# More rounds of filling products, one result copy on ScalarE, and the last value load in three pieces

## The chip, the cores and the metric

The kernel runs on one core of a Trainium2 chip. TensorE (PE in the profile) multiplies, and its weight loads are listed as PEld; VectorE (DVE), ScalarE (ACT) and GpSimd (POOL) work on tiles in on-chip memory; the sequencer of SyncE (SP) issues nearly all DMA transfers. Each engine has a sequencer of its own that also runs loop counters, register arithmetic, branches and semaphore waits; the profile gives its instructions a q (PEldq is TensorE's). The metric is the device time of one execution in microseconds (us). The kernel before takes 1368.91 us, the median of three runs from 1368.70 to 1369.06.

## The reference: two attention decodes

Two independent attentions, A and B, each for one new token in four sequences. Cut to what matters:

```python
def _A_ref(x, k_cache, v_cache, wq, wo):          # 32 query heads on 8 key heads
    q = (x @ wq) as (B, 32, 1, 128)
    k, v = the last W = 2048 positions of the caches, each head used four times
    p = softmax(q . k * 128 ** -0.5)
    return (p . v) as (B, 1, 4096) @ wo

def _B_ref(x, k_cache, v_cache, wq, wo):          # 32 heads, all 8192 positions
    q = (x @ wq) as (B, 32, 1, 128)
    p = softmax(q . k_cache * 128 ** -0.5)
    return (p . v_cache) as (B, 1, 4096) @ wo

return concatenate([a, b], axis=-1)               # (4, 1, 1024)
```

All inputs are bf16. B's two caches are by far the largest part of the bytes read.

## The kernel before

The work is cut into chunks. A has 8 chunks, each one key head for all four sequences. B has 32, each four heads of one sequence: 256 key tiles and 256 value tiles of 128 by 128, 8.4 MB of each. Here a chunk of B is called y, from 0 to 31. B's chunks 0, 4, 8, ... 28 begin a group of four that share one load of the output weights (`wos`, 0.5 MB).

The order of the work is written out by hand. `_Sched` keeps one list of operations for each engine, with the keys that each operation waits for. `emit_looped` finds equal stretches of a list and emits them as a hardware loop; on TensorE one such loop covers the chunks of B, so there is one copy of a B chunk in TensorE's program, and what differs from chunk to chunk is computed from the loop's register.

`whole_B` (L982) is one chunk of B on all engines. In order of TensorE:

- `reorder`: 16 products that bring the chunk's output weights from `wos` into the wanted order (in PSUM banks `tr` and `po`). `take_wol` copies them to `wol` with VectorE and ScalarE.
- `more_busy` (L947): the filling products, whose result (bank `sc`) nobody reads. A round is `BUSYBODY` = 3 products of 128 by 512. They stand in a loop of their own, a `Fori` whose end is an expression in the chunk's number (L961). That gives `MOREBUSY` + 1 = 4 rounds for y from 2 to 28 and one round for the others.
- For each of 32 groups of 8 key tiles, `emit_T` transposes the tiles (L519, `tr<-identb,kv`), VectorE or ScalarE copies them to `kt`, and two groups later `emit_S` multiplies them with the query (L521, `sc<-qq,kt`). The first group waits for the chunk's keys to land. Maxima and exponentials of the first half are put in between.
- `emit_pv`: 256 products of value tiles with probabilities, the first 128 into `po`, the other 128 into `tr`, with the statistics of the second half between them. At the tile groups listed in `QV` it waits for that part of the value tiles to have landed.
- `norm_sum`, `add_first`, `norm_out` and `emit_fin` scale the result and multiply it with the output weights (bank `fin`).

The loads are in one queue of SP (L498 to L504): for each chunk the keys, then the values, and after the last chunk two pieces of A's output weights (`dma_wo`, chunks 6 and 7 of A). The key buffer holds one chunk and the value buffer holds one chunk. The keys of chunk y + 1 are asked for when the first 128 key tiles of chunk y have been transposed; the values of chunk y + 1 when the value products of chunk y are done with that part. GpSimd passes on that a piece has landed (L85, `relay`) and copies half of a chunk's keys to a spare place (L440) in chunks whose keys come as one piece. Most loads are one piece of 256 tiles. Those of the last chunk are cut up: `LASTV` gives its values in pieces of 128, 64, 48 and 16 tiles.

After the last chunk, two products close bank `fin` for B, the last A chunks' products with the output weights follow, and `emit_out` (L891) copies each result from `fin` to `outsb` on VectorE and issues two output DMAs, one from ACT's queue and one from SP's. B's copy comes first, then A's last products, then A's copy.

Of the kernel before, what the change touches and what calls it, by code (L numbers as in the profile page):

```python
# [7 lines left out]
ACTF = mybir.ActivationFunctionType  # L8
# [21 lines left out]
QUARTERS = (64, 64, 64, 64)  # L30
NLATE = 4
NEXTV = (128, 64, 64)
LASTV = (128, 64, 48, 16)
QK = (0, 4, 8)
QC = (16, 24)
QV = (0, 8, 16, 24, 30)
NBUSY = 0
BUSYBODY = 3
MOREBUSY = 3
FILL = (6, 3)  # L40

TRM0, BC0, L0, Q0, XT0 = 0, 256, 288, 320, 448
# [146 lines left out]
def bass_concat_heads__sliding_block_cached__mha_block_cached__decode_kernel(  # L189
# [6 lines left out]
    DO = A_wo.shape[1]  # L196
# [33 lines left out]
    chunks.append(dict(chunks[NCA]))  # L230
    assert all(sum(x) == NTB for x in (LASTV, NEXTV, ENDK, QUARTERS, HALVES, WHOLE)) and NTA * 16 == 1024 and NTB * 4 == 1024
    NCP = (NTB - KMAIN) // TG

    sch = _Sched()
    with ExitStack() as es:
        block = es.enter_context(nc.Block())

        def sb(name, shape, dt):
            return es.enter_context(nc.sbuf_tensor(name, shape, dt))

        def ps(name, shape, dt):
            return es.enter_context(nc.psum_tensor(name, shape, dt))
# [38 lines left out]
        outsb = sb("outsb", [P, DO // 2], BF16)  # L281
# [9 lines left out]
        fin = ps("fin", [P, 512], F32)  # L291
# [22 lines left out]
            waits=["c_onesf", "c_identf"], key="c_ind")  # L314
# [85 lines left out]
        def vpieces(c):  # L400
            return LASTV if c == NC - 1 else NEXTV if c == NC - 2 else HALVES if c <= NCA + 2 or c == NC - 3 else WHOLE

# [64 lines left out]
        def land_vB(c):  # L467
# [3 lines left out]
            for i, m in enumerate(pieces):  # L471
                sch.relay("pool", sems, "r_v", m // TG, [("v", c, i)])
            for g, end in zip(QV, QV[1:] + (NTB // TG,)):
                sch.tk[("vr", c, g)] = ("r_v", n * (NTB // TG) + end)
# [290 lines left out]
        def emit_pv(c, g):  # L765
# [3 lines left out]
            for t in range(TG):  # L769
# [11 lines left out]
                if j == 0:  # L781
                    po_read[:] = []
                waits += [("vr", c, g)] if t == 0 and g in QV else []
                o = (po2 if h else po)[:, 0:NW]
# [103 lines left out]
        def out_halves(ab):  # L888
            return [(64 * (1 - ab) + 32 * h, slice(h * DO // 2, (h + 1) * DO // 2)) for h in (0, 1)]

        def emit_out(c):  # L891
            ab = 0 if c < NCA else 1
            at = out_halves(ab)
            rows = slice(at[0][0], at[1][0] + NB)
            sch.add("dve", lambda e: e.tensor_copy(outsb[rows, :], fin[rows, 0:DO // 2]), waits=[("end", 32) if ab else ("fin", c)], key=("osb", ab))
            for h, (p0, x) in enumerate(at):
                sch.add_dma("sp" if h else "act", lambda e, x=x, p0=p0: e.dma_start(out[:, 0, ab * DO + x.start:ab * DO + x.stop], outsb[p0:p0 + NB, :]),
                            "d_out", waits=[("osb", ab)], key=("out", ab, h))
# [48 lines left out]
        def more_busy(c):  # L947

            n = c - NCA

            def mm(e):
                return e.matmul(sc[:, 1, :], identb[:, :], sel4[:, :, :].rearrange("p r x -> p (r x)"), start=True, stop=True)  # L952

            def emit(e, x=0):
                if isinstance(e, _Record):
                    return mm(e)
                if isinstance(x, int):
                    for _ in range(BUSYBODY):
                        mm(e)
                    return None  # L960
                with nc.Fori(0, (((x + n + 30) >> 5) - ((x + n + 3) >> 5)) * MOREBUSY + 1, 1, engines=type(mybir.ALL_ENGINES)([mybir.EngineType.PE])):  # L961
                    for _ in range(BUSYBODY):
                        mm(e)
                return None

            sch.add("pe", emit, at=n)
# [96 lines left out]
        for c in range(NCA - LATEWO, NCA - 1):  # L1063
            emit_fin(c)
        emit_out(NC - 1)
        emit_fin(NCA - 1)
        emit_out(NCA - 1)

        @block.sync
# [56 lines left out]
```

## Time and profile before

| | |
|---|---|
| three timed runs, median | 1368.91 us |
| the profiled execution, its own time | 1368.63 us |
| its span, first to last instruction | 1366.9 us |
| mean granted TensorE clock | 0.984 |
| read from HBM | 587.21 MB |
| TensorE busy | 1222.5 us, 89% |
| VectorE, ScalarE, GpSimd busy | 731.2, 555.0, 202.8 us |
| filling products (L952), weight loads | 339, 30.6 us |

The profile shows one execution. Times in its views count from the first instruction; the execution's own time is 1.7 us longer than its span. A row of a timeline has the start, the length, the engine, the line of the program and what was written from what, with the idle time ahead of it and what ended that in brackets. `x` counts the instructions taken together. A row of one source line gives shortest, median and longest duration in ns, and the first and last start in us.

### The profile page before, as it was taken

The numbers are of one execution on the slowest core, as the hardware profiler recorded it, in microseconds if no ns is written. First come the engines' busy times: TensorE is split into PE (matmuls) and PEld (weight loads), VectorE is DVE, ScalarE is ACT, GpSimd is POOL, SyncE is SP. The second block draws the span as 40 slices with busy tenths as digits, with TensorE's granted clock in tenths as the row PEclk, the third lists the DMA queues.
The fourth block names the chain that finished last, engine by engine and source line by source line (L and its number), as shares of the span: only waits on it lengthen the run. The fifth ranks groups of instructions, "written<-read, shape, count | busy, mean of one in ns | idle before, by whom it ended". The sixth has DMA issues, their size and how long they took to land.

```text
span 1366.9 us, 62986 instructions
## 1 busy us (share of the span) xinstructions
PE 1222.5 (89%) x27834; PEld 1127.1 (82%) x27951; DVE 731.2 (53%) x1495; ACT 555.0 (41%) x777; POOL 202.8 (15%) x84
## 2 busy tenths in 40 slices
PE   6688799989998999989999899989999899999998
PEld 5688798878888988878889888878898888888888
DVE  2575355545555555545555555545555555455555
ACT  2353344334344443433444444334444343344443
POOL 2000022222210222222101222221022222200000
PEclk9998899999999999999999999999999999999999
DMA  9999999999999999999999999999999999999998
GB/s 398 427 428 431 430 439 432 438 433 428 433 433 426 441 433 433 426 432 443 432 430 430 441 432 432 432 433 435 433 432 430 439 433 432 430 439 420 433 424 368
DMA packets 16772, 587.51 MB, mean 430 GB/s; under 512 B 1880, under 2 KB 2032, under 8 KB 4208
## 3 DMA queue, kind: packets, MB, share of 16 engines
q1 hardware_dynamic: 16720, 587.21, 99.7%
q8 instruction: 15, 0.25, 0.1%
q14 instruction: 5, 0.04, 0.0%
q10 hardware_dynamic: 32, 0.01, 0.0%
HBM read 587.21 MB, written 0.01 MB: 430 GB/s over the span
## 4 chain that ended last, share of the span: by engine, by line
DMA 64%; PE 32%; DVE 1%; issue 1%; ACT 1%; SPq 0%; POOLq 0%; ACTq 0%; DVEq 0%
DMA kv<-in_B_k_cache_dram 58%; PE tr L519 20%; PE sc L521 9%; DMA kv<-in_A_k_cache_dram 4%; DMA kv<-in_B_v_cache_dram 3%; PE tr L521 2%; PE po L521 1%; PE ms L521 0%; DVE sA L649 0%; ACT pba L748 0%; PE sc L952 0%; ACT kt L594 0%; PE fin L521 0%; DVE kt L596 0%; ACT pbb L718 0%
## 5 line engine op out<-in xcount | busy, mean ns | idle before, releaser
L519 PE MATMUL tr<-identb,kv 128*128 128x128 bf16 x8704 | 662.1, 221 | 60.2 <-POOLq L85 49.8
L596 DVE COPY kt<-tr 128x1024 bf16<-128x1024 bf16 x736 | 502.2, 691 | 320.9 <-PE tr L519 317.8
L519 PEld LDWEIGHTS tr<-identb,kv 128*128 128x128 bf16 x8704 | 511.7, 99 | 77.0 <-issue 68.7
L594 ACT ACTIVATE kt<-tr 128x1024 bf16<-128x1024 bf16 x352 | 359.3, 1023 | 457.0 <-PE tr L519 454.8
L521 PE MATMUL sc<-qq,kt 128*128 128x64 bf16 x8192 | 398.9, 192 | 11.4 <-DVE kt L596 9.5
L521 PEld LDWEIGHTS sc<-qq,kt 128*128 128x128 bf16 x8192 | 327.9, 98 | 18.5 <-DVE kt L596 12.7
L440 POOL COPY kv<-kv 128x4096 int32<-128x4096 int32 x54 | 192.9, 3602 | 988.2 <-DMA kv<-in_B_k_cache_dram 988.2
L718 ACT ACTIVATE pbb<-sc,negb 32x128 bf16<-32x128 f32 x256 | 137.9, 539 | 134.2 <-DVE negb L700 131.4
L521 PE MATMUL tr<-pbb,kv 128*128 128x64 bf16 x4096 | 137.1, 194 | 27.1 <-ACT pbb L718 25.5
L521 PEld LDWEIGHTS tr<-pbb,kv 128*128 128x128 bf16 x4096 | 132.4, 100 | 30.9 <-issue 28.6
L521 PE MATMUL po<-pbb,kv 128*128 128x64 bf16 x4096 | 135.1, 194 | 2.9 <-issue 2.4
L521 PEld LDWEIGHTS po<-pbb,kv 128*128 128x128 bf16 x4096 | 127.5, 98 | 4.0 <-issue 2.5
L866 ACT ACTIVATE wol<-tr 128x512 bf16<-128x512 f32 x32 | 19.1, 597 | 201.4 <-PE po L521 201.4
L952 PE MATMUL sc<-sel,identb 128*128 128x512 bf16 x226 | 67.7, 381 | 9.5 <-issue 5.2
L868 DVE CAST wol<-tr 128x512 bf16<-128x512 f32 x64 | 41.2, 686 | 54.7 <-PE tr L521 54.7
L952 PEld LDWEIGHTS sc<-sel,identb 128*128 128x128 bf16 x339 | 30.6, 98 | 46.6 <-issue 14.2
L725 DVE TENSOR_REDUCE rs<-pbb 128x4 f32<-128x512 bf16 x32 | 22.0, 686 | 50.1 <-ACT pbb L718 50.1
L798 DVE RECIPROCAL ib<-ms 128x8 f32<-128x8 f32 x32 | 6.7, 208 | 58.8 <-PE ms L521 58.8
L521 PE MATMUL tr<-wos,back 32*128 32x512 bf16 x384 | 34.8, 383 | 0.5 <-issue 0.5
L521 PE MATMUL po<-wos,back 32*128 32x512 bf16 x128 | 33.9, 385 | 0.0
L686 DVE TENSOR_REDUCE gm<-ms 4x4 f32<-4x128 f32 x72 | 19.8, 275 | 25.0 <-PE ms L519 25.0
L666 DVE TENSOR_REDUCE rh<-sc 128x4 f32<-128x512 f32 x32 | 22.1, 692 | 14.3 <-PE sc L521 14.3
(90 smaller groups left out, 490.1 us busy)
## 6 DMA issues: line engine op xcount, KB each, us to landing
kv<-in_B_v_cache_dram SPq DMA_DIRECT2D x10, 4096.0 KB, 25.2
kv<-in_B_k_cache_dram SPq DMA_DIRECT2D x7, 4096.0 KB, 21.7
kv<-in_A_k_cache_dram SPq DMA_DIRECT2D x8, 2048.0 KB, 15.7
kv<-in_A_v_cache_dram SPq DMA_DIRECT2D x8, 2048.0 KB, 16.9
kv<-in_B_k_cache_dram SPq DMA_DIRECT2D x6, 2048.0 KB, 27.1
kv<-in_B_v_cache_dram SPq DMA_DIRECT2D x3, 2048.0 KB, 30.9
kv<-in_A_wq_dram SPq DMA_DIRECT2D x1, 4096.0 KB, 12.4
kv<-in_B_wq_dram SPq DMA_DIRECT2D x1, 4096.0 KB, 22.8
```

The lines of the kernel that those rows point to most:

```text
L440: sch.add("pool", lambda e, dst=dst, org=org: e.tensor_copy(dst, org), waits=[("T", s0 + ch["NG"] - 1)] if g == QC[0] else [])
L519: sch.add("pe", lambda e: e.transpose(o, l, r), waits, key)
L521: sch.add("pe", lambda e: e.matmul(o, l, r, start=start, stop=stop), waits, key)
L594: sch.add("act", lambda e: e.activation(dst, src, ACTF.Copy), waits=waits, key=("ev", s))
L596: sch.add("dve", lambda e: e.tensor_copy(dst, src), waits=waits, key=("ev", s))
L666: sch.add("dve", lambda e: e.tensor_reduce(out=dst, in_=src, axis=AX.X, op=ALU.max), waits=[("S", ch["s"] + (half + 1) * ch["NG"] // 2 - 1 ...
L686: sch.add("dve", lambda e: e.tensor_reduce(out=gm[0:C, m, 0:U], in_=src, axis=AX.X, op=ALU.max), waits=[key_of("trm", c, half)], key=key_o ...
L718: sch.add("act", lambda e, src=src, dst=dst, pp=pp, u=u: e.activation(dst, src, ACTF.Exp, bias=negb[pp, half, u:u + 1], scale=scale), wait ...
L725: sch.add("dve", lambda e: e.tensor_reduce(out=dst, in_=probs_of(c, half).rearrange("p j u -> p u j"), axis=AX.X, op=ALU.add), waits=[("ex ...
L866: sch.add("act", lambda e, u=u, o=o: e.activation(wol[:, u, :], o, ACTF.Copy), waits=[("reord", c, u)], key=("wol", c, u))
L868: sch.add("dve", lambda e, u=u, o=o: e.tensor_copy(wol[:, u, :], o), waits=[("reord", c, u)], key=("wol", c, u))
L952: return e.matmul(sc[:, 1, :], identb[:, :], sel4[:, :, :].rearrange("p r x -> p (r x)"), start=True, stop=True)
```

## The change: the diff

Three edits. The number of rounds of filling products goes from four to five for y from 2 to 28, and to seven for y = 4, 8, 12, 16, 20 and 24; the expression for the loop's end gets a second term, `first`, that is 1 for those six chunks and 0 for the others. B's result is copied to `outsb` by ScalarE; A's copy stays on VectorE. The last chunk's values come in three pieces of 128, 88 and 40 tiles, and the last place at which the value products wait moves from group 30 to group 27, in all chunks.

```diff
-LASTV = (128, 64, 48, 16)
+LASTV = (128, 88, 40)
...
-QV = (0, 8, 16, 24, 30)
+QV = (0, 8, 16, 24, 27)
...
-MOREBUSY = 3
+MOREBUSY = 4
+GROUPBUSY = 2
...
-            sch.add("dve", lambda e: e.tensor_copy(outsb[rows, :], fin[rows, 0:DO // 2]), waits=[("end", 32) if ab else ("fin", c)], key=("osb", ab))
+            waits = [("end", 32) if ab else ("fin", c)]
+            if ab:
+                sch.add("act", lambda e: e.activation(outsb[rows, :], fin[rows, 0:DO // 2], ACTF.Copy), waits=waits, key=("osb", ab))
+            else:
+                sch.add("dve", lambda e: e.tensor_copy(outsb[rows, :], fin[rows, 0:DO // 2]), waits=waits, key=("osb", ab))
...
-                with nc.Fori(0, (((x + n + 30) >> 5) - ((x + n + 3) >> 5)) * MOREBUSY + 1, 1, engines=type(mybir.ALL_ENGINES)([mybir.EngineType.PE])):
+                y = x + n
+                first = ((y >> 2) - ((y + 3) >> 2) + ((y + 31) >> 5) - ((y + 4) >> 5) + 33 >> 1) - 16
+                with nc.Fori(0, (((y + 30) >> 5) - ((y + 3) >> 5)) * MOREBUSY + first * GROUPBUSY + 1, 1, engines=type(mybir.ALL_ENGINES)([mybir.EngineType.PE])):
                     for _ in range(BUSYBODY):
                         mm(e)
```

## The prediction

> **What bounds the kernel now.** I read the page first, then the chain of waits.
>
> ```profile
> span 1366.9 us, 62986 instructions
> ...
> PEclk9998899999999999999999999999999999999999
> DMA  9999999999999999999999999999999999999998
> ...
> DMA 64%; PE 32%; DVE 1%; issue 1%; ACT 1%; SPq 0%; POOLq 0%; ACTq 0%; DVEq 0%
> ...
> 1118.47 28.08 DMA kv<-in_B_k_cache_dram
> 1157.17 28.07 DMA kv<-in_B_k_cache_dram
> ```
>
> The DMA engines are busy in every slice. A chunk's keys are asked for every 1157.17 - 1118.47 = 38.70 us, in which 16.8 MB of keys and values come in, 433 GB/s; they land 28 us after they are asked for, of which their own bytes need 19.4 us, so something is always queued ahead of them. The kernel before is bound by the transfers. The 32% of PE in the chain is the work that frees a buffer while the queue is still full.
>
> So the question is how far TensorE is from becoming the bound. The timeline of TensorE's weight loads and the chain give it, around an ordinary chunk (y = 27), one that begins a group (y = 24), and at y = 1 and 28:
>
> ```profile
> 1179.91 0.17 PEld L521 LDWEIGHTS tr<-wos,back 32*128 32x128 bf16 x6 [0.26 <-issue]
> ...
> 1185.41 1.34 PEld L519 LDWEIGHTS tr<-identb,kv 128*128 128x128 bf16 x24 [2.19 <-issue]
> ...
> 1218.61 0.16 PEld L521 LDWEIGHTS tr<-wos,back 32*128 32x128 bf16 x6 [0.26 <-issue]
> ...
> 1062.52 0.17 PEld L521 LDWEIGHTS tr<-wos,back 32*128 32x128 bf16 x6 [0.26 <-issue]
> ...
> 1069.30 1.34 PEld L519 LDWEIGHTS tr<-identb,kv 128*128 128x128 bf16 x24 [3.47 <-issue]
> ...
> 171.35 1.51 PE tr L519 x24
> ...
> 1222.42 1.34 PE tr L519 x24
> ```
>
> From its first transpose to the reorder of the next chunk TensorE takes 1218.61 - 1185.41 = 33.20 us. From the reorder to the transposes there are 5.50 us in an ordinary chunk and 6.78 us in one that begins a group (its `wos` load delays the keys). In these lie the reorder, the filling, and the wait for the keys. Chunk 28, with its keys in pieces, already follows without a wait.
>
> **The change part by part.** The filling first. Its products are cheap; what matters is who counts the rounds. The rows of L961, over the whole span, over chunk 27 and over one of its rounds, and two other rows of register arithmetic:
>
> ```profile
> L961 PEldq FUSED_REGOPS  x226: 37/120/228, 121.6 to 1327.1; - x113
> L961 PEldq COMPARE_BRANCH  x113: 69/201/212, 122.0 to 1327.1; - x113
> L961 PEldq MOVE  x32: 29/29/34, 121.5 to 1326.7; - x32
> ...
> L961 PEldq FUSED_REGOPS  x8: 37/117/207, 1180.1 to 1182.3; - x8
> L961 PEldq COMPARE_BRANCH  x4: 69/201/201, 1180.5 to 1182.4; - x4
> ...
> L961 PEldq FUSED_REGOPS  x2: 37/117/197, 1181.4 to 1181.7; - x2
> L961 PEldq COMPARE_BRANCH  x1: 201/201/201, 1181.8 to 1181.8; - x1
> ...
> L123 PEldq FUSED_REGOPS  x102: 37/37/42, 37.4 to 1351.0; - x102
> ...
> L605 ACTq FUSED_REGOPS  x32: 60/60/60, 116.5 to 1320.1; - x32
> ...
> 1181.18 2.54 PE L952 MATMUL sc<-sel,identb 128*128 128x512 bf16 x8 [0.16 <-issue]
> ```
>
> The counter is set 32 times, once a chunk (MOVE), but there are 113 branches and 226 = 2 x 113 arithmetic instructions: 27 chunks of 4 rounds and 5 of one. **The loop's end is worked out anew in every round.** The branches of chunk 27 go from 1180.5 to 1182.4, three periods of 0.63 us. That happens to be the time of the products themselves (12 in 2.54 us, 0.21 us each, 0.63 us a round), so in the kernel before the sequencer just keeps up and its work can't be seen.
>
> The old end has 8 steps: the counter's own, y + 30, shift, y + 3, shift, a subtraction, times MOREBUSY, plus 1. An instruction with a product and a sum (L123) takes 37 ns, so the 37 ns one is the last two steps, and the 197 ns one holds six, two of them shifts. The new end adds 15 steps for `first`, five of them shifts: 23 steps, 7 shifts. They don't appear in the trace; I price them from these rows. A simple step: (60 - 37)/2 = 11.5 ns, from L605, which has two steps more than L123, though on another engine. The rest of an instruction: 37 - 23 = 14 ns. A shift, with whatever the six-step instruction takes beyond that: (197 - 14 - 4 x 11.5)/2 = 68 ns. With six steps to an instruction 23 steps need four, with some 60 ns between two (from the start at 1181.4 to the branch at 1181.8 less 234 ns, over two gaps; an estimate). New: 7 x 68 + 16 x 11.5 + 4 x 14 = 716 ns. A round of the sequencer is then 0.63 - 0.23 + 0.72 + 2 x 0.06 = **1.24 us**, about twice its products.
>
> Both ends of this price: below, if all 17 steps after the first six cost like simple ones, 197 + 17 x 11.5 + 3 x 14 = 435 ns, a round of 0.95 us; above, if all four instructions take the 207 ns of the longest in chunk 27, 828 ns, a round of 1.35 us. I stay near 1.24, because five of the added steps are shifts, and keep both ends.
>
> The sequencer reaches the transposes 0.25 us plus its rounds after the reorder's first load (0.2 us to the first arithmetic instruction at 1180.1, the rest for the wait's own; four rounds of 0.63 us give 2.8 us, in line with the last branch at 1182.4 and two short instructions). Five rounds: 0.25 + 5 x 1.24 = 6.45 us, 0.95 us more than the 5.50 there are. Seven: 8.93 us, 2.15 us more than 6.78. The transposes no longer wait for keys, they are late, and with them every engine and every release of a buffer: TensorE is the bound. Nothing is given back, since the 33.20 us hold no wait for a transfer. From y = 2 to 28 there are 21 chunks of five rounds and 6 of seven: 27 x 33.20 + 21 x 6.45 + 6 x 8.93 = 1085.4 us, from the transposes of chunk 1, which still wait for keys (171.35), to those of chunk 28 at 1256.8, against 1222.42: **+34.3 us**. The last three chunks have one round, covered by the copies to `wol`.
>
> Some waits further on fall away then:
>
> ```profile
> 1257.30 1.49 PE tr L519 x24
> ...
> 1293.39 1.51 PE tr L519 x24
> ...
> 1328.42 1.51 PE L519 MATMUL tr<-identb,kv 128*128 128x128 bf16 x24
> ...
> 1325.78 0.17 DVE L832 TENSOR_TENSOR oz<-tr,rz 128x16 bf16<-128x16 f32 x1 [1.13 <-PE tr L521]
> ...
> 1362.94 0.17 DVE L832 TENSOR_TENSOR oz<-tr,rz 128x16 bf16<-128x16 f32 x1 [1.13 <-PE tr L521]
> ```
>
> Chunk 29 takes 1293.39 - 1257.30 = 36.09 us, chunk 30 takes 35.03: 1.06 us of waiting for keys. From transposes to `oz` chunk 30 takes 32.39 us, the last 34.52: 2.13 us of waiting for values. A late TensorE finds both landed: -3.2 us.
>
> **The last values in three pieces.** Landings after the issues at 1325.78, 1326.15 and 1326.62, and the second half's products:
>
> ```profile
> kv<-in_B_v_cache_dram SPq DMA_DIRECT2D x1, 2048.0 KB, 30.9
> kv<-in_B_v_cache_dram SPq DMA_DIRECT2D x1, 1536.0 KB, 34.2
> kv<-in_B_v_cache_dram SPq DMA_DIRECT2D x1, 512.0 KB, 35.0
> ...
> 1357.09 2.04 PE L521 MATMUL tr<-pbb,kv 128*128 128x64 bf16 x64 [0.82 <-ACT pbb L718]
> ```
>
> So tiles are there at 1356.7, 1360.3 and 1361.6. A piece of 88 lands half way between the first two, at 1358.5; 88 products of 32 ns and the norm's 0.2 us end at 1361.5, the last 40 wait for 1361.7 and end at 1363.1, against `oz` at 1362.94: +0.2 us at most if transfers still set the end, nothing if they don't.
>
> **B's copy on ScalarE.**
>
> ```profile
> 1363.95 0.42 DVE L895 CAST outsb<-fin 36x256 bf16<-36x256 f32 x1 [0.84 <-PE fin L521]
> ...
> 1364.63 0.43 DVE L895 CAST outsb<-fin 36x256 bf16<-36x256 f32 x1 [0.27 <-PE fin L521]
> ...
> L866 ACT ACTIVATE wol<-tr 128x512 bf16<-128x512 f32 x32 | 19.1, 597 | 201.4 <-PE po L521 201.4
> ```
>
> The second copy waits for TensorE, not for the first. On ScalarE the first is at most the 0.6 us of a tile twice as wide; behind it stand only two output issues, the second of which needs A's copy (to 1365.06) anyway. Nothing, both ways within 0.1 us.
>
> **Sum.** 34.3 - 3.2 = +31.1 us on the profiled execution's 1368.6 (span 1366.9 and 1.7 around it; the median of the runs, 1368.9, is 0.3 above): 1399.7, say **1400 us**.
>
> [...]
>
> **Rivals.** *The count costs nothing*: the sequencer runs far enough ahead of the products, or the end is worked out once a chunk. Place: the filling; it decides where a round takes no more than (5.50 - 0.25)/5 = 1.05 us. Then five rounds fit, what the six long ones lose the next chunk's wait takes up, and with the tail's 0.2 us the time is 1368.8. For it: the first products wait behind the reorder, so the sequencer is about 1 us ahead, and the low end of my price is 0.95. Against: x226 for x113, and a lead of 1 us is used up within two rounds. Not slower, 8%.
>
> *The clock drops as well*:
>
> ```profile
> 280.00:300.00 20.00, 16.44 (x287) 14.11 (x287) 8.29 (x15) 5.18 (x6) 7.15 (x2) 0.91 1.04 449
> ...
> 1180.00:1200.00 20.00, 17.98 (x360) 15.99 (x364) 11.51 (x18) 8.01 (x9) 7.14 (x2) 1.00 1.01 439
> ...
> 288.89 2.58 PE tr L519 x24
> ```
>
> After the long wait ahead of y = 4 the granted clock is 0.91 in its slice and the first 24 transposes take 2.58 us, not 1.51. If half-empty filling counted as idle, each of 27 chunks would lose about 1.1 us: +29 us, 1429. Against: no gap would exceed 0.6 us. 9%. [...]
>
> *It does what it says*: the waits filled, the clock kept, TensorE earlier. That would be faster only if TensorE set the end; the transfers do, and the tail gives 0.2 us at best. 1%.
>
> **How the numbers follow.** The forecast has 82%. Each 0.1 us of a round is 147 rounds x 0.1 = 14.7 us: 1.08 us gives 1376, 1.35 gives 1416; with part of the clock's rival I take 1376 to 1420. This kernel's measurement tells 0.2% from no change, 2.7 us. Slower: 82 + 9%, rounded to 0.91. Same: 0.08. Faster: 0.01.
>
> **What would show it.** Right: L961 has 27 x 5 + 6 x 2 + 5 = 152 branches and some four arithmetic instructions to each; the branches of a chunk stand 1.2 us apart; the gaps ahead of the transposes end by TensorE's own sequencer and not by POOL's relay; the DMA row falls below 9 in the slices of B; `oz` follows the last values without a wait. Wrong: two arithmetic instructions a round, or transposes that still wait for keys.

## The result and the profile after

The changed kernel takes **1405.82 us** (median of 6 runs, 1405.75 to 1407.28) against 1368.88 for the kernel before (6 runs): a ratio of 1.0272, with a 95% interval from 1.0262 to 1.0282. The profiled execution took 1406.03 us, 37.4 more than the one before. Its page and its chain of waits:

```profile
span 1404.3 us, 63600 instructions
...
PEclk8998999999999999999999999999999999999999
DMA  9999999999999999999999999999999999999998
...
PE 78%; issue 9%; DMA 6%; DVE 3%; ACT 2%; ACTq 0%; SPq 0%; POOLq 0%; DVEq 0%
...
L520 PE MATMUL tr<-identb,kv 128*128 128x128 bf16 x8704 | 658.5, 220 | 23.2 <-issue 14.0
L957 PE MATMUL sc<-sel,identb 128*128 128x512 bf16 x304 | 90.9, 381 | 64.3 <-issue 62.9
```

The same two rows of the kernel before:

```profile
L519 PE MATMUL tr<-identb,kv 128*128 128x128 bf16 x8704 | 662.1, 221 | 60.2 <-POOLq L85 49.8
L952 PE MATMUL sc<-sel,identb 128*128 128x512 bf16 x226 | 67.7, 381 | 9.5 <-issue 5.2
```

The chain that was 64% DMA is now 78% PE and 9% "issue", time in which TensorE waited for nothing that the profile shows. About half of that 9% (some 126 us) lies ahead of the filling products, where TensorE was idle for 62.9 us with no releaser in sight, against 5.2 before. Ahead of the transposes it had waited 49.8 us for GpSimd's word that keys had landed (L85); now the largest part of a shorter wait is issue. The DMA row still reads 9 throughout; it can't show the loss.

The loop's own instructions, over the span, in the five rounds of one chunk (y = 6), and in one of these rounds:

```profile
L968 PEldq FUSED_REGOPS  x608: 96/200/262, 121.8 to 1367.2; - x152
L968 PEldq COMPARE_BRANCH  x152: 75/207/212, 122.8 to 1367.3; - x152
...
L968 PEldq FUSED_REGOPS  x20: 96/200/256, 366.8 to 372.7; - x20
L968 PEldq COMPARE_BRANCH  x5: 75/207/207, 367.8 to 372.9; - x5
...
L968 PEldq FUSED_REGOPS  x4: 96/198/246, 369.3 to 370.1; - x4
```

There are 152 rounds, and 608 = 4 x 152 arithmetic instructions, where the kernel before had two to a round. The last row's four take 197, 246, 200 and 96 ns. The branches of the chunk go from 367.8 to 372.9, four periods of 1.27 us.

The same chunk in TensorE's weight loads, from the reorder to the transposes, with the next reorder:

```profile
366.55 0.16 PEld L522 LDWEIGHTS tr<-wos,back 32*128 32x128 bf16 x6 [0.26 <-issue]
...
367.58 0.98 PEld L957 LDWEIGHTS sc<-sel,identb 128*128 128x128 bf16 x6 [0.42 <-issue]
369.31 0.33 PEld L957 LDWEIGHTS sc<-sel,identb 128*128 128x128 bf16 x3 [0.75 <-issue]
370.61 0.33 PEld L957 LDWEIGHTS sc<-sel,identb 128*128 128x128 bf16 x3 [0.97 <-issue]
371.86 0.33 PEld L957 LDWEIGHTS sc<-sel,identb 128*128 128x128 bf16 x3 [0.93 <-issue]
373.18 1.34 PEld L520 LDWEIGHTS tr<-identb,kv 128*128 128x128 bf16 x24 [0.99 <-issue]
...
406.37 0.16 PEld L522 LDWEIGHTS tr<-wos,back 32*128 32x128 bf16 x6 [0.26 <-issue]
...
373.19 1.01 PE L520 MATMUL tr<-identb,kv 128*128 128x128 bf16 x15 [0.50 <-issue]
...
368.94 7.14 POOL L441 COPY kv<-kv 128x4096 int32<-128x4096 int32 x2 [33.93 <-DMA kv<-in_B_k_cache_dram]
```

And in the kernel before the filling and the transposes of chunk 27:

```profile
1180.95 2.27 PEld L952 LDWEIGHTS sc<-sel,identb 128*128 128x128 bf16 x12 [0.42 <-issue]
...
1185.41 1.51 PE L519 MATMUL tr<-identb,kv 128*128 128x128 bf16 x24 [1.70 <-POOLq L85]
```

In the kernel before, the filling was one row of 12 weight loads without a gap. In the changed kernel the first two rounds run on together, because the sequencer starts about 1 us ahead (its first arithmetic instruction is at 366.8, the first weight load of the filling at 367.58 and its first product at 367.81). From the third round on the weight loads of each wait 0.75 to 0.97 us, and those of the transposes 0.99 us, for nothing but their own issue. The transposes start at 373.18, 6.63 us after the reorder, where the kernel before needed 5.50 and was held by the keys. The row of GpSimd (POOL) shows that the keys are not what is late: it copies part of them from 368.94 on, when they have landed, 4.2 us ahead of the transposes.

### The profile page after: what moved, and what is told of

Its sections match the earlier page's. It is cut to its first block, busy times and chain, and to the rows that moved or that the text cites. A ratio compares the mean times of both kernels' runs of the same rounds, so it can differ in the third digit from the quotient of the medians.

```text
span 1404.3 us, 63600 instructions
## 1 busy us (share of the span) xinstructions
PE 1239.6 (88%) x27912; PEld 1124.1 (80%) x28068; DVE 730.3 (52%) x1494; ACT 555.5 (40%) x778; POOL 202.8 (14%) x84
## 3 DMA queue, kind: packets, MB, share of 16 engines
q1 hardware_dynamic: 16576, 587.21, 98.4%
HBM read 587.21 MB, written 0.01 MB: 418 GB/s over the span
## 4 chain that ended last, share of the span: by engine, by line
PE 78%; issue 9%; DMA 6%; DVE 3%; ACT 2%; ACTq 0%; SPq 0%; POOLq 0%; DVEq 0%
PE tr L520 34%; PE sc L522 17%; PE tr L522 12%; PE sc L957 6%; PE po L522 5%; DMA kv<-in_A_k_cache_dram 4%; DMA kv<-in_B_k_cache_dram 2%; PE ms L522 2%; ACT pbb L719 2%; DVE kt L597 2%; PE fin L522 1%; PE ms L520 1%; DVE sA L650 0%; DVE oz L833 0%; DVE negb L701 0%
## 5 line engine op out<-in xcount | busy, mean ns | idle before, releaser
L957 PE MATMUL sc<-sel,identb 128*128 128x512 bf16 x304 | 90.9, 381 | 64.3 <-issue 62.9
L957 PEld LDWEIGHTS sc<-sel,identb 128*128 128x128 bf16 x456 | 34.4, 97 | 121.1 <-issue 96.8
## 6 DMA issues: line engine op xcount, KB each, us to landing
kv<-in_B_wq_dram SPq DMA_DIRECT2D x1, 4096.0 KB, 21.8
```

## The experiments

The theory: TensorE's sequencer works the loop's end out anew in every round, the longer end makes a round 1.27 us and not 0.64, and the rounds no longer fit into the wait. Rival 1: TensorE has no room for the added products themselves. Rival 2: one of the other two edits costs the time. Each experiment's own median stands beside that of the kernel before on the same chip, 1368.54 us for the first four, 1368.62 for the others; a ratio is that of the means of all runs, so it can differ a little from that of the medians. "The end" is the expression for the end of the filling's loop: the old end is that of the kernel before, the long end that of the changed kernel.

**The end worked out once a chunk.** Same rounds, same products:

```diff
-                with nc.Fori(0, (((y + 30) >> 5) - ((y + 3) >> 5)) * MOREBUSY + first * GROUPBUSY + 1, 1, engines=type(mybir.ALL_ENGINES)([mybir.EngineType.PE])):
+                end = e.compute_val((((y + 30) >> 5) - ((y + 3) >> 5)) * MOREBUSY + first * GROUPBUSY + 1)
+                with nc.Fori(0, end, 1, engines=type(mybir.ALL_ENGINES)([mybir.EngineType.PE])):
```

> The changed kernel, with the loop's end worked out once a chunk, ahead of the loop, and kept in a register; five and seven rounds as before. Theory (the count is worked out in every round, and TensorE's sequencer sets the pace): a round falls back to its products, 0.64 us; five of them end 4.5 us after the reorder, seven 5.8 us, inside the 5.50 and 6.78 us that the keys leave. 1368.9 us, 1368.5 to 1369.6. Rival 1 (the added products themselves are what TensorE has no room for): the same number of products, so 1406. Rival 2 (one of the other two edits costs it): 1406.

Measured: 1368.95 us, ratio 1.0005 (0.9995 to 1.0015). The arithmetic's rows (L968) and the loop's (L969), the filling's and the transposes' weight loads of chunk 27, and the page's row of the transposes:

```profile
L968 PEldq FUSED_REGOPS  x96: 207/225/263, 121.5 to 1327.2; - x96
L968 PEldq ALU_OP  x32: 36/36/36, 122.4 to 1327.5; - x32
...
L969 PEldq ALU_OP  x152: 32/36/36, 122.6 to 1327.7; - x152
L969 PEldq COMPARE_BRANCH  x152: 76/208/218, 122.7 to 1327.8; - x152
...
1180.97 2.93 PEld L957 LDWEIGHTS sc<-sel,identb 128*128 128x128 bf16 x15 [0.56 <-issue]
1185.30 1.34 PEld L520 LDWEIGHTS tr<-identb,kv 128*128 128x128 bf16 x24 [1.40 <-issue]
...
L520 PE MATMUL tr<-identb,kv 128*128 128x128 bf16 x8704 | 656.6, 220 | 35.6 <-POOLq L86 26.1
```

There are still 152 rounds, but the end is worked out 32 times, once a chunk, in three long instructions and a short one; what is left in each round is the counter's own step (ALU_OP, 36 ns) and the branch. The 15 weight loads follow one another without a gap, and the transposes wait for keys again (26.1 us for L86, GpSimd's relay). The whole loss is gone with the products all there. Rivals 1 and 2 are out.

**More products with the old end.** Six rounds for y from 2 to 28:

```diff
-MOREBUSY = 4
-GROUPBUSY = 2
+MOREBUSY = 5
...
-                first = ((y >> 2) - ((y + 3) >> 2) + ((y + 31) >> 5) - ((y + 4) >> 5) + 33 >> 1) - 16
-                with nc.Fori(0, (((y + 30) >> 5) - ((y + 3) >> 5)) * MOREBUSY + first * GROUPBUSY + 1, 1, engines=type(mybir.ALL_ENGINES)([mybir.EngineType.PE])):
+                with nc.Fori(0, (((y + 30) >> 5) - ((y + 3) >> 5)) * MOREBUSY + 1, 1, engines=type(mybir.ALL_ENGINES)([mybir.EngineType.PE])):
```

> The changed kernel, with the old expression for the loop's end and six rounds for y from 2 to 28: 167 rounds in all, 15 more than the changed kernel. Theory: a round of 0.64 us; six end 5.1 us after the reorder, inside 5.50. 1368.9 us, 1368.5 to 1369.6. Rival 1 (products): more products than the changed kernel, so slower than it, about 1409. Rival 2 (the other edits): 1406.

Measured: 1369.41 us, ratio 1.0007 (0.9998 to 1.0017). The loop's rows:

```profile
L966 PEldq FUSED_REGOPS  x334: 37/120/225, 121.6 to 1327.3; - x167
L966 PEldq COMPARE_BRANCH  x167: 69/201/212, 121.9 to 1327.4; - x167
```

With 167 rounds, 15 more than the changed kernel, and two arithmetic instructions to each as in the kernel before, it is within 0.2% of the kernel before.

**The long end, with four rounds and with five.** The constant 32 makes `first` 0 in chunks 2 to 28 and leaves every step in (in chunks 29 to 31 it makes it -1; they still run one round):

```diff
-                first = ((y >> 2) - ((y + 3) >> 2) + ((y + 31) >> 5) - ((y + 4) >> 5) + 33 >> 1) - 16
+                first = ((y >> 2) - ((y + 3) >> 2) + ((y + 31) >> 5) - ((y + 4) >> 5) + 32 >> 1) - 16
...
-MOREBUSY = 4
+MOREBUSY = 3
```

The second of the two kernels leaves MOREBUSY at 4.

> The changed kernel's count (its constant 33 made 32, so that the second term is 0 in chunks 2 to 28, with the same steps) and four rounds as in the kernel before. Theory: the changed kernel's trace has 6.63 us for five rounds, 1.28 us each; four end 5.35 us after the reorder, 0.15 us inside the 5.50: no loss in chunks 2 to 27, 1.5 us in chunk 28, of which the later waits take most. 1369.2 us, 1368.7 to 1370.5. If the sequencer's lateness costs even when it fits, some 1375 or more. Rival 1 (products): 1369, as before. Rival 2: 1406.

> The same count (constant 32) and five rounds in every chunk from 2 to 28, none with seven. Theory: 27 chunks of 33.20 + 6.63 us from the transposes of chunk 1, +24.7 us at chunk 28, less the 3.2 us of waits that fall away: 1390.4 us, 1388 to 1392. Rival 1 (products): 15 rounds of 4 are added per 39 of the changed kernel, 69% of its loss, 1394. Rival 2: 1406.

Measured: four rounds 1369.06 us, ratio 1.0004 (0.9994 to 1.0013); five rounds 1390.31 us, ratio 1.0162 (1.0145 to 1.0179). The record's "15 rounds of 4" for rival 1 is a slip: 27 of the 39 added rounds are meant, which is its 69%. Three successive chunks of the five-round kernel in its chain:

```profile
370.38 1.51 PE tr L520 x24
410.23 1.51 PE tr L520 x24
450.08 1.51 PE tr L520 x24
```

A chunk takes 39.85 us, 33.19 of fixed work and 6.63 of reorder and filling. The last of the three is y = 8, to which the changed kernel gives seven rounds; with five it comes as soon as its neighbours. The kernel before needs (1222.42 - 171.35)/27 = 38.93 us on average, so 27 x 0.92 = 24.8 us are lost, less the 3.2 us of later waits 21.6; measured are 21.8. Rival 1 had 1394 for this kernel. And the cost doesn't grow from the first long round on: four of them just fill the 5.50 us (5.51 us from reorder to transposes in chunk 27 of the four-round kernel) and cost nothing that can be measured.

**Longer rounds with the long end in each.** Rounds of six products, three and four of them:

```diff
-BUSYBODY = 3
-MOREBUSY = 4
-GROUPBUSY = 2
+BUSYBODY = 6
+MOREBUSY = 2
+GROUPBUSY = 1
```

> The changed kernel with its count in every round, but rounds of six products: three rounds for most chunks, four for the six, one for the others, so 18 and 24 products where the changed kernel has 15 and 21. Theory (a round takes the longer of its products and its count, here 1.28 us and about 1.3 us): three rounds end 4.3 us after the reorder on the sequencer and 5.1 us on TensorE, inside 5.50; four 5.6 and 6.4, inside 6.78. In chunks 28 to 31 some 1.3 us and three times 0.7 us are added, of which the later waits take nearly all: 1369.5 us, 1368.6 to 1371. Rival 1 (products): more of them than in the changed kernel, 1409 or more. Rival 3 (each evaluation of the count costs its 0.6 us wherever it stands): 87 of them in chunks 2 to 28, more than the waits can take, over 1375.

Measured: 1368.84 us, ratio 1.0001 (0.9991 to 1.0011). The three rounds of chunk 27 in the loop's rows, that chunk's weight loads, and the page's row of the transposes:

```profile
L968 PEldq FUSED_REGOPS  x9: 198/225/262, 1180.0 to 1183.2; - x9
L968 PEldq ALU_OP  x3: 36/36/36, 1180.9 to 1183.4; - x3
L968 PEldq COMPARE_BRANCH  x3: 82/213/213, 1181.0 to 1183.5; - x3
...
1180.88 3.57 PEld L957 LDWEIGHTS sc<-sel,identb 128*128 128x128 bf16 x18 [0.42 <-issue]
1185.30 1.34 PEld L520 LDWEIGHTS tr<-identb,kv 128*128 128x128 bf16 x24 [0.86 <-issue]
...
L520 PE MATMUL tr<-identb,kv 128*128 128x128 bf16 x8704 | 655.9, 220 | 24.5 <-POOLq L86 11.5
```

The end is worked out in every round, in three long instructions and one short ALU_OP of 36 ns, where the changed kernel's fourth takes 96 ns; no run shows why. The branches stand (1183.5 - 1181.0)/2 = 1.25 us apart, about as in the changed kernel, but a round's products now take about 1.28 us (six of 0.21 us each), so it just hides. With 18 products where the changed kernel has 15, the transposes wait for keys (L86). Rival 3, a price for each evaluation wherever it stands, is out: a round takes the longer of the two.

**The other two edits alone**, each in the kernel before:

```diff
-LASTV = (128, 64, 48, 16)
+LASTV = (128, 88, 40)
...
-QV = (0, 8, 16, 24, 30)
+QV = (0, 8, 16, 24, 27)
```

> The kernel before with the last values in pieces of 128, 88 and 40 tiles alone (LASTV and QV). Theory: the products of the second half wait for the 88-tile piece, the last 40 end 0.2 us later than the last 16 did: 1368.7 us, within 0.5 us of the kernel before; in the trace oz of the last chunk 0.1 to 0.3 us later. Rival (fewer and larger pieces land earlier): up to 0.5 us faster. Either is below what the times can tell; the trace tells.

```diff
-            sch.add("dve", lambda e: e.tensor_copy(outsb[rows, :], fin[rows, 0:DO // 2]), waits=[("end", 32) if ab else ("fin", c)], key=("osb", ab))
+            waits = [("end", 32) if ab else ("fin", c)]
+            if ab:
+                sch.add("act", lambda e: e.activation(outsb[rows, :], fin[rows, 0:DO // 2], ACTF.Copy), waits=waits, key=("osb", ab))
+            else:
+                sch.add("dve", lambda e: e.tensor_copy(outsb[rows, :], fin[rows, 0:DO // 2]), waits=waits, key=("osb", ab))
```

> The kernel before with B's copy on ScalarE alone. Theory: A's copy still waits for TensorE's last product, so nothing changes: 1368.5 us, within 0.4 us of the kernel before; the copy takes 0.3 to 0.6 us and ends before A's copy does. Rival (it delays the issue of A's first output): up to 0.5 us slower.

Measured: the three pieces 1368.96 us, ratio 1.0003 (0.9994 to 1.0012); the copy 1368.59 us, ratio 0.9998 (0.9989 to 1.0007). The three pieces in the timeline of the last chunk, then the copies of the other kernel:

```profile
1358.44 1.75 PE L521 MATMUL tr<-pbb,kv 128*128 128x64 bf16 x54 [2.27 <-POOLq L85]
...
1363.12 0.17 DVE L832 TENSOR_TENSOR oz<-tr,rz 128x16 bf16<-128x16 f32 x1 [1.43 <-PE tr L521]
```

```profile
1363.74 0.38 ACT L897 ACTIVATE outsb<-fin 36x256 bf16<-36x256 f32 x1 [6.76 <-PE fin L521]
...
1364.42 0.43 DVE L899 CAST outsb<-fin 36x256 bf16<-36x256 f32 x1 [1.51 <-PE fin L521]
```

The second half's products wait until 1358.44, for the larger piece, where they began at 1357.09; `oz` comes at 1363.12, 0.18 us later than in the kernel before. ScalarE's copy takes 0.38 us and is done at 1364.12, 0.3 us before A's copy can start. Both land where the expectation put them, below what the times can tell.

**What the filling is worth at all.** The kernel before with one round in every chunk:

```diff
-MOREBUSY = 3
+MOREBUSY = 0
```

> The kernel before with one round of filling in every chunk. Theory (transfers set the time, TensorE has room even at the lower clock): the waits ahead of the transposes grow by 1.9 us, the granted clock drops after many of them, each time some 1.1 to 1.6 us of TensorE's time, less than the wait: mean clock below 0.97 and the time the same, 1368.5 us, 1368.1 to 1369.5. Rival (the filling earns its place, a dropped clock makes TensorE late): over 1371.

Measured: 1369.33 us, ratio 1.0011 (1.0000 to 1.0022). Two of its slices:

```profile
280.00:300.00 20.00, 16.36 (x329) 14.77 (x326) 8.90 (x17) 5.18 (x6) 7.15 (x2) 0.91 1.01 436
320.00:340.00 20.00, 17.64 (x360) 16.05 (x357) 9.65 (x18) 6.20 (x7) 7.14 (x2) 0.91 0.99 423
```

The clock's column (the third from the end) reads 0.91 in these two, the mean clock is 0.965, and the profiled execution takes 1368.40 us: the theory holds there. But the ten runs go from 1368.40 to 1374.99, three of them above 1371, where the rival has them. None of the 33 runs of the kernel before that go with it is above 1370.46. So the filling doesn't make this kernel faster in most executions; it seems to keep some from being slower. The three have the lowest mean clocks of the ten, 0.956 to 0.963 against 0.964 to 0.970, which fits the rival, but none of them is the profiled one, and the cause stays open.

**The filling that fits, with the old ending.** The end worked out once a chunk as in the first experiment, five and seven rounds, copy and last values as in the kernel before:

> Five and seven rounds with the end worked out once a chunk, and the copy and the last values as in the kernel before. Theory: the filling now fits its waits and keeps the clock, but transfers set the time: 1368.5 us, within 0.5 us of the kernel before, mean clock 0.988 or more. If a kept clock were worth something, 1367.5 or less.

Measured: 1368.50 us, ratio 0.9997 (0.9988 to 1.0006), clock 0.991. It is the fastest form that was run, and the same as the kernel before within its interval.

## Why the prediction was right, step by step

- **The mechanism** was right: the long end in each round, rounds twice as long as their products, transposes late, TensorE the bound. The first experiment takes exactly the arithmetic in each round away, and nothing measurable is left of the loss.
- **The round** was the term that came out too small: 1.24 us forecast, 1.27 in the branches and (6.63 - 0.25)/5 = 1.28 in the path to the transposes. The four arithmetic instructions take 197 + 246 + 200 + 96 = 739 ns, not 716; the branch takes 207 ns, and the remaining 0.32 us of the 1.27 lie between these instructions. That the sum of the four came within some 3% is in part luck: the price of a simple step came from ScalarE's sequencer, and no run prices a single step inside a long instruction. Nor is it known which steps stand in which instruction. The forecast put at most six into one; but the first experiment works out the 22 steps that are left without the counter's in three long instructions and one short one of 36 ns, which is what the counter's single step takes, and 3 x 6 + 1 is only 19. Either more than six go into one, or some steps are merged.
- **From reorder to transposes**: 6.63 us for five rounds where I had 6.45. For seven the reorder of y = 8 and its transposes give 455.41 - 446.20 = 9.21 where I had 8.93:

```profile
446.20 0.16 PEld L522 LDWEIGHTS tr<-wos,back 32*128 32x128 bf16 x6 [0.26 <-issue]
...
455.41 0.67 PEld L520 LDWEIGHTS tr<-identb,kv 128*128 128x128 bf16 x12 [0.99 <-issue]
```

- **The fixed 33.20 us** held: 406.37 - 373.18 = 33.19. So did the claim that nothing is given back on the way.
- **The sum.** The transposes of chunks 1 and 28 to 31, and the last `oz`:

```profile
171.50 1.51 PE tr L520 x24
...
1262.80 1.51 PE tr L520 x24
1297.85 1.48 PE tr L520 x24
1332.92 1.48 PE tr L520 x24
1367.97 1.49 PE tr L520 x24
...
1400.34 0.17 DVE L833 TENSOR_TENSOR oz<-tr,rz 128x16 bf16<-128x16 f32 x1 [1.13 <-PE tr L522]
```

  Chunk 28 is 1262.80 - 1222.42 = 40.4 us later, not 34.3; the 6 us are the round's 0.04 us, 147 times. Chunk 29 takes 35.07 us, so the 1.0 us of waiting for keys fell away, and from its transposes to `oz` the last takes 32.37 us, 2.15 less: the 3.2 us as forecast. 40.4 - 3.2 = 37.2 of the 37.4 us measured.
- **The clock's rival** is out: rounds that are half empty kept the clock. In the chain the first 24 transposes take 1.51 us in every chunk from 2 to 28. The slice at y = 4, where the wait for keys was among the longest, now has 1.00 and 1.51 us, where the kernel before had 0.91 and 2.58:

```profile
280.00:300.00 20.00, 15.84 (x293) 12.14 (x297) 6.31 (x15) 3.95 (x5) 7.14 (x2) 1.00 1.02 436
...
293.49 1.51 PE tr L520 x24
```

  The longest gap of TensorE's products in the filling is 0.7 us. How long a pause brings the clock down was not shown; the pauses of the kernel before don't settle it. At y = 4 its clock was down (0.91 in the slice) after TensorE's products had paused for 2.98 us, and at y = 24 it was not (1.00) after a pause of the same 2.98 us:

```profile
288.89 2.58 PE L519 MATMUL tr<-identb,kv 128*128 128x128 bf16 x24 [2.98 <-POOLq L85]
...
1069.31 1.51 PE L519 MATMUL tr<-identb,kv 128*128 128x128 bf16 x24 [2.98 <-POOLq L85]
...
1060.00:1080.00 20.00, 16.44 (x329) 14.04 (x330) 9.00 (x18) 6.10 (x7) 7.15 (x2) 1.00 0.98 423
```

- **The two small edits** cost what was worked out: in the kernel before 0.18 us where 0.2 at most was forecast, and nothing.
- **One sign was wrong**: the DMA row was to fall below 9. It stays at 9, although 418 GB/s come in and no longer 430.

## What to carry to other kernels

A loop's end written as an expression can be worked out in every round; count its register instructions against the rounds in the profile (two to each of 113 here, four to each of 152 after). They were invisible here as long as they were shorter than the round's work (the sequencer's round of 1.25 us against 1.28 us of products, 1368.84 us in all), or the wait behind the loop had room for them (four long-ended rounds, 1369.06 us); the step from four long-ended rounds to five then cost 27 x 0.8 us at once. Compute the end once ahead of the loop (1368.95 us), or make the rounds longer. And ask first what filling can gain: here, where the transfers set the time, rounds that fit gave the time of the kernel before (1368.50 us against 1368.62).

## What the runs showed that was not expected

The busy share of the DMA engines said little here about the room they had left. Over one chunk of the kernel before and over 40 us of the changed kernel:

```profile
1146.70:1185.40 38.70, 35.29 (x810) 32.47 (x814) 20.83 (x41) 15.82 (x22) 7.15 (x2) 1.00 1.00 434
```

```profile
333.00:373.00 40.00, 35.89 (x812) 32.51 (x817) 20.82 (x41) 15.82 (x22) 6.07 (x3) 1.00 0.98 419
```

The rate falls by 3.5%, the share from 1.00 to 0.98. For the same 587.21 MB the time that packets are counted for grew by 1.4%: the page gives 99.7% of 1366.9 us before and 98.4% of 1404.3 us after. Why the same bytes are counted for longer when they came in more slowly, no run shows.
